# Converting weights beside a fused attention and FFN kernel: sign words and first merges of 24 blocks in PSUM instead of SBUF

## Chip, cores and metric

The kernel runs on one core of one Trainium2 chip. The metric is the device time in microseconds of one execution; of several runs the median is given. One core has the matrix engine (PE, with its weight loads as PEld), the vector engine (DVE), the scalar engine (ACT), GpSimd (POOL) and the sync engine (SP), which here issues the DMAs. Each engine works through its own instructions in order and waits on semaphores. SBUF is the large on-chip memory; PSUM has eight banks of 2 KB per partition, into which PE writes its products, and which DVE and ACT can read and write too.

## The reference

The first half is attention over 8 batches with 8 heads, 512 local and 32 global tokens, and heads of 64. A global query sees every key; a local query sees the 32 global keys and the local keys within 32 positions. The result, 4608 tokens of 512 numbers, goes through a gated FFN:

```python
k_all = np.concatenate([k_g, k_l], axis=2)
out_g = np.matmul(sm(scale * q_g @ k_all^T), v_all)
s_ll = np.where(np.abs(pos[:, None] - pos[None, :]) <= 32, scale * q_l @ k_l^T, -1e9)
out_l = np.matmul(sm(concat([scale * q_l @ k_g^T, s_ll])), concat([v_g, v_l]))
...
gate = 1.0 / (1.0 + np.exp(-(x @ w_gate)))
val = x @ w_val
return (gate * val @ w_out).astype(np.float32)
```

w_gate and w_val are 512 x 1536, w_out is 1536 x 512. All three arrive as 64-bit floating-point numbers.

## The kernel before

**Tiling.** Tokens are worked in ten chunks: the first batch in two halves of 256 tokens (chunks 0 and 1), each further batch as one chunk of 512, and all global tokens as a last chunk of 256. For each chunk attention computes x, by units of two 128-row query blocks of one head (local_unit) and one unit of 32 global queries per head (global_unit). A unit is a chain over PE, DVE and ACT: scores (L237, L317), their negated maximum and masking on DVE (L251, L322), exp on ACT (L254, L326), scaling by the reciprocal sum (L225 on DVE, L223 on ACT; p_buf, p_first and pg_buf are the scaled scores), transposes on PE (L268, L335), and products with v (L290, L291, L348).

The FFN (ffn_stream) has one item per chunk and per slice f of 128 of the 1536 inner columns: twelve matmuls each for gate and value (L380; three products of a high and a low part over four row tiles), the gate function on ACT and DVE (L388 to L399), a split of the result in a high part on ACT (L401) and a low part on POOL (L402), and the output products (L415), which collect in the PSUM banks bank_o0 to bank_o3 over all twelve f. Chunk 0 collects in bank_o0 and bank_o1, chunk 1 in bank_o2 and bank_o3, a chunk of 512 in all four. The other four banks (tag att) are for everything else. The items come in this order: eight of chunk 0 (f from 0 to 7), eight of chunk 1, the rest of both in turn, then the whole chunks.

**The weight blocks.** The 64-bit weights are converted on the chip, in 36 blocks: for each f one block of w_gate (number 3f), one of w_val (3f + 1) and one of w_out (3f + 2), each of 128 partitions x 512 numbers. A block's raw words come by DMA into one of three staging buffers; one of two buffers v takes the 32-bit result. Of each number there is a low and a high word, lying side by side, so the operations read with a step of two. On a block there are, in convert:

- L140, DVE: the sign bit of the high word into v ("sign words" below)
- L146 on DVE or L144 on ACT, in turn: the high word scaled in place, which puts the exponent right
- L147, DVE: the low word shifted right and merged into v ("first merge")
- L148, DVE: the high word shifted left and merged into v ("second merge")
- L149, ACT: the high part of v, rounded, into the weight tile
- L150, POOL: v minus the high part, the low part

Since there are two buffers v, a block's L140 waits until POOL has done L150 of the block two before. The staging buffer is free for the next load after the second merge.

**What sets the order.** A list of events with times in units of FFN work (att_events, CONVERT, START) gives the order in which the program is written; the compiler's scheduler then arranges each engine's instructions by readiness, so the order on an engine also follows the lengths it expects. Blocks of f = 0 come during the attention of chunk 0, the others at four units per f.

At the start PE has nothing to multiply for some time and runs filler matmuls (fill, L113) into a tile in bank_o3: eight, and then one at a unit's steps of chunk 0. One filler has two records in the trace.

Of the kernel before, what the change touches and what calls it, by code (L numbers as in the profile page):

```python
# [10 lines left out]
U32 = mybir.dt.uint32  # L11
AF = mybir.ActivationFunctionType
ALU = mybir.AluOpType
# [4 lines left out]
P = 128  # L18
# [12 lines left out]
DM = 512  # L31
# [25 lines left out]
def kernel(ctx, tc, qk, v, w_gate, w_val, w_out, out_l, out_g):  # L57
    nc = tc.nc
# [12 lines left out]
    ps = ctx.enter_context(tc.tile_pool(name="ps", bufs=1, space=PSUM))  # L71
# [53 lines left out]
    def stage(i):  # L125
        if i < len(w_src):
            src = w_src[i]
            st = conv_bufs[0][i % len(conv_bufs[0])].rearrange("p (t n) -> p t n", t=src.shape[1])
            nc.sync.dma_start(st, src)

    def convert(i, hi, lo):

        src = w_src[i]
        t, n = src.shape[1], src.shape[2] // 2
        st, v = (o[i % len(o)].rearrange("p (t n) -> p t n", t=t) for o in conv_bufs)
        words = st.rearrange("p t (n two) -> p t n two", two=2)
        low, high = words[:, :, :, 0], words[:, :, :, 1]
        vf, hf = v.bitcast(F32), high.bitcast(F32)
        with tc.issue_after(anchor[0].ins) if i < 3 else nullcontext():
            nc.vector.tensor_scalar(v, high, 0x80000000, None, op0=ALU.bitwise_and)  # L140


            if REBASE[i % len(REBASE)] == "s":
                nc.scalar.mul(hf, hf, 2.0 ** -112)  # L144
            else:
                nc.vector.tensor_scalar(hf, hf, 2.0 ** -112, None, op0=ALU.mult)  # L146
            nc.vector.scalar_tensor_tensor(v, low, 29, v, op0=ALU.logical_shift_right, op1=ALU.bitwise_or)  # L147
            nc.vector.scalar_tensor_tensor(v, high, 3, v, op0=ALU.logical_shift_left, op1=ALU.bitwise_or)  # L148
        nc.scalar.copy(hi, vf)  # L149
        nc.gpsimd.tensor_tensor(lo, vf, hi.bitcast(F32), op=ALU.subtract)  # L150
        stage(i + len(conv_bufs[0]))

    def convert_w(f, i):
        fs = slice(f * P, (f + 1) * P)
        w = (wg, wv)[i]
        convert(3 * f + i, w[0][:, :, fs], w[1][:, :, fs])

    def convert_wo(f):
        hi, lo = (spl.tile([P, 1, DM], F32R, name=nm, tag="kl") for nm in ("wo_hi", "wo_lo"))
        convert(3 * f + 2, hi, lo)  # L160
        nc.sync.dma_start(wo_dram[f][:, 0], hi[:, 0].bitcast(F32))
        nc.sync.dma_start(wo_dram[f][:, 1], lo[:, 0].bitcast(F32))
# [420 lines left out]
```

## Time and profile before

| | us |
|---|---|
| median of three runs | 1246.45 |
| lowest and highest | 1245.38 and 1247.57 |
| the profiled execution | 1240.82 |
| its span, from first to last instruction | 1238.9 |
| PE busy in the span | 1216.7 (98%) |
| DVE busy | 845.0 (68%) |
| ACT busy | 780.6 (63%) |
| POOL busy | 564.2 (46%) |

All durations and places quoted below are from the one profiled execution; its times count from the start of the span. Busy time counts instructions from start to end, with whatever they wait for once they have begun. PE's ends are modelled from a pipeline, so that a full PE isn't always a PE at its peak; the granted clock tells at which rate it was allowed to run. An engine's instruction can be recorded up to some 0.08 us before the previous one has ended, so starts tell how fast a queue moves. A line number such as L140 is that of the kernel before; in the changed kernel the lines behind the edit stand six further down (L140 is L146 there, L147 and L148 are L153 and L154).

### The profile page before, as it was taken

What the parts mean: (1) busy time and instruction counts of PE and PEld (TensorE: products, weight loads), DVE (VectorE), ACT (ScalarE), POOL (GpSimd) and SP (SyncE); (2) the same over time, 40 slices, a digit from 0 to 9 for tenths busy, and PEclk for the clock granted to TensorE, in tenths of its full rate; (3) what the DMA queues carried; (4) which work ended last, traced back from release to release, by engine and by line L of the source; (5) the groups of instructions that cost most, each with busy time, mean ns of one, the idle gap of its engine ahead of it and who ended that gap; (6) DMA issues with size and microseconds to landing.
All of it is one profiled execution on the core that took longest, in us unless ns stands there. A gap on an engine that the chain in (4) does not pass through costs nothing.

```text
span 1238.9 us, 20551 instructions
## 1 busy us (share of the span) xinstructions
PE 1216.7 (98%) x6884; PEld 998.4 (81%) x6884; DVE 845.0 (68%) x2433; ACT 780.6 (63%) x1899; POOL 564.2 (46%) x573
## 2 busy tenths in 40 slices
PE   8898999999999999999999999999999999999998
PEld 6677778888888788888888888888888788888897
DVE  6899976757776777767776777767776777622232
ACT  4786777756765676656765776657675666533333
POOL 2345455635554455535554555535554555311111
PEclk9898999999999999999999999999999999999999
DMA  6778754333433433433333333333433332121243
GB/s 228 230 261 251 252 169 135 110 99 96 112 90 111 131 98 100 112 118 110 94 109 107 107 105 110 94 115 109 110 93 124 106 97 81 52 93 61 68 137 120
DMA packets 59498, 151.90 MB, mean 123 GB/s; under 512 B 6144, under 2 KB 19456, under 8 KB 59392
## 3 DMA queue, kind: packets, MB, share of 16 engines
q1 hardware_dynamic: 59392, 150.59, 40.5%
q8 instruction: 54, 0.88, 0.3%
q14 instruction: 52, 0.43, 0.1%
HBM read 135.36 MB, written 15.20 MB: 122 GB/s over the span
## 4 chain that ended last, share of the span: by engine, by line
PE 82%; DVE 8%; issue 5%; ACT 2%; POOL 2%; DMA 0%; POOLq 0%; DVEq 0%; ACTq 0%
PE bank_v L380 21%; PE bank_g L380 20%; PE bank_o L415 20%; PE bank_x L237 5%; PE bank_y L268 5%; PE bank_x L348 2%; DVE p_buf L225 2%; PE bank_x L317 2%; PE bank_y L335 2%; PE bank_x L298 2%; PE bank_x L299 2%; DVE xt L148 1%; POOL hh L402 1%; PE bank_x L290 1%; DVE pt L280 1%
## 5 line engine op out<-in xcount | busy, mean ns | idle before, releaser
L380 PE MATMUL bank_g<-xt,wg 128*128 128x512 f32 (+1 forms) x1440 | 337.1, 369 | 0.9 <-DVE th L399 0.5
L380 PE MATMUL bank_v<-xt,wv 128*128 128x512 f32 (+1 forms) x1440 | 334.7, 370 | 0.2 <-ACT pg_buf L326 0.2
L415 PE MATMUL bank_o<-wo,hh 128*128 128x512 f32 x1224 | 334.3, 404 | 0.4 <-ACT hh L401 0.4
L380 PEld LDWEIGHTS bank_v<-xt,wv 128*128 128x128 f32 x1440 | 238.5, 191 | 38.7 <-issue 2.0
L380 PEld LDWEIGHTS bank_g<-xt,wg 128*128 128x128 f32 x1440 | 236.6, 190 | 40.1 <-issue 3.2
L415 PEld LDWEIGHTS bank_o<-wo,hh 128*128 128x128 f32 x1224 | 215.0, 189 | 38.2 <-ACT hh L401 0.9
L402 POOL TENSOR_TENSOR hh<-th,hh 128x512 fp32r<-128x512 f32 (+1 forms) x120 | 137.9, 1149 | 212.1 <-ACT hh L401 198.1
L254 ACT ACTIVATE s_sb<-s_sb,nm 128x224 f32<-128x224 f32 x240 | 113.7, 474 | 90.8 <-DVE nm L251 90.4
L225 DVE TENSOR_SCALAR p_buf<-s_sb,r 128x128 f32<-128x128 f32 (+1 forms) x443 | 157.7, 401 | 8.0 <-PE bank_y L268 4.5
L206 POOL TENSOR_TENSOR kl<-qk_raw,qk_hi 128x704 fp32r<-128x704 f32 x52 | 88.3, 1698 | 135.1 <-ACT qk_hi L205 135.1
L393 DVE TENSOR_SCALAR mn<-bank_g 128x512 f32<-128x512 f32 (+1 forms) x108 | 67.2, 622 | 103.0 <-ACT th L388 101.5
L388 ACT ACTIVATE th<-bank_g 128x512 f32<-128x512 f32 (+1 forms) x120 | 63.4, 528 | 95.1 <-PE bank_g L380 92.3
L401 ACT CAST hh<-th 128x512 fp32r<-128x512 f32 (+1 forms) x120 | 66.6, 555 | 89.0 <-DVE th L399 89.0
L303 POOL TENSOR_TENSOR x<-t 64x256 f32<-64x256 f32 x104 | 76.2, 733 | 99.7 <-DVE t L302 96.5
L398 DVE TENSOR_TENSOR bank_v<-bank_v,mn 128x512 f32<-128x512 f32 (+1 forms) x120 | 73.3, 611 | 44.4 <-PE bank_v L380 37.7
L251 DVE CUSTOM_DVE_ANT_0 s_sb<-bank_x,masks 128x224 f32<-128x224 f32 x240 | 84.3, 382 | 19.8 <-PE bank_x L237 15.6
L218 POOL TENSOR_TENSOR vhl<-v_raw,vhl 128x512 fp32r<-128x512 f32 x52 | 67.7, 1301 | 59.0 <-ACT vhl L217 58.1
L205 ACT CAST qk_hi<-qk_raw 128x1248 fp32r<-128x1248 f32 x52 | 64.1, 1233 | 36.6 <-PE bank_y L319 36.5
L208 POOL TENSOR_TENSOR qk_hi<-qk_raw,qk_hi 64x256 fp32r<-64x256 f32 x104 | 82.6, 814 | 4.1
L268 PE MATMUL bank_y<-ident,p_buf 128*128 128x128 f32 x496 | 78.3, 279 | 5.8 <-DVE p_buf L225 4.0
L268 PEld LDWEIGHTS bank_y<-ident,p_buf 128*128 128x128 f32 x496 | 58.6, 141 | 28.3 <-ACT pg_buf L326 9.4
L280 DVE TENSOR_TENSOR pt<-bank_y,pt 128x512 fp32r<-128x512 f32 x104 | 70.5, 678 | 14.7 <-ACT pt L279 14.7
(111 smaller groups left out, 1940.7 us busy)
## 6 DMA issues: line engine op xcount, KB each, us to landing
wo<-wo_dram SPq DMA_DIRECT2D x116, 512.0 KB, 3.6
qk_raw<-in_qk_dram SPq DMA_DIRECT2D x104, 312.0 KB, 4.3
v_raw<-in_v_dram SPq DMA_DIRECT2D x52, 256.0 KB, 2.6
out_dram<-ob SPq DMA_DIRECT2D x34, 256.0 KB, 2.7
xt<-in_w_gate_dram SPq DMA_DIRECT2D x12, 512.0 KB, 4.7
xt<-in_w_val_dram SPq DMA_DIRECT2D x12, 512.0 KB, 4.7
xt<-in_w_out_dram SPq DMA_DIRECT2D x12, 512.0 KB, 4.7
v_nat<-in_v_dram SPq DMA_DIRECT2D x8, 512.0 KB, 4.6
```

What stands on the lines that cost most here:

```text
L206: nc.gpsimd.tensor_tensor(kl, t[:, K0:Q1], hi[:, K0:Q1].bitcast(F32), op=ALU.subtract)
L208: nc.gpsimd.tensor_tensor(hi[64:128, r], t[64:128, r], hi[64:128, r].bitcast(F32), op=ALU.subtract)
L225: nc.vector.tensor_scalar(out, in_, by, None, op0=ALU.mult)
L251: anchor[0] = nc.vector.tensor_tensor_reduce(out=s_sb[:, i], in0=s_ps[:, i, 0:WIN], in1=masks[:, m], scale=-0.125, scalar=3.0e38, op0=ALU. ...
L254: nc.scalar.activation(s_sb[:, i], s_sb[:, i], AF.Exp, bias=nm[:, i:i + 1], scale=-1.0, accum_out=sm[:, i:i + 1])
L268: nc.tensor.transpose(pt_ps[:, 2 * i + t], pb[:, i, t * P:(t + 1) * P], ident)
L280: nc.vector.tensor_tensor(pt[:, 1], pt_ps, pt[:, 0].bitcast(F32), op=ALU.subtract)
L303: nc.gpsimd.tensor_tensor(dst, t0[:, :, 0], t0[:, :, 1], op=ALU.add)
L380: nc.tensor.matmul(acc, w[a][:, t, fs], xt[:, c, t, x0:x0 + ntok], start=n == 0, stop=n == 11)
L398: nc.vector.tensor_tensor(acc, acc, mn, op=ALU.mult)
L402: nc.gpsimd.tensor_tensor(hh[:, 1, 0:ntok], th, hh[:, 0, 0:ntok].bitcast(F32), op=ALU.subtract)
L415: nc.tensor.matmul(o_ps[t], ph[:, a, t * P:(t + 1) * P], pwo[:, c], start=f2 == 0 and i == 0, stop=f2 == NF - 1 and i == 2)
```

## The change

For the first 24 blocks (f from 0 to 7) a tile u of one PSUM bank is taken, bank_o2 for even and bank_o3 for odd blocks. The sign words go into u, the first merge reads and writes u, and the second merge reads u and writes v in SBUF. The in-place scaling, ACT's and POOL's steps and the other twelve blocks are as before.

```diff
         with tc.issue_after(anchor[0].ins) if i < 3 else nullcontext():
-            nc.vector.tensor_scalar(v, high, 0x80000000, None, op0=ALU.bitwise_and)
+            if i < 24:
+                u = ps.tile([P, DM], U32, name="bank_o%d" % (2 + i % 2)).rearrange("p (t n) -> p t n", t=t)
+            else:
+                u = v
+            nc.vector.tensor_scalar(u, high, 0x80000000, None, op0=ALU.bitwise_and)
...
-            nc.vector.scalar_tensor_tensor(v, low, 29, v, op0=ALU.logical_shift_right, op1=ALU.bitwise_or)
-            nc.vector.scalar_tensor_tensor(v, high, 3, v, op0=ALU.logical_shift_left, op1=ALU.bitwise_or)
+            nc.vector.scalar_tensor_tensor(u, low, 29, u, op0=ALU.logical_shift_right, op1=ALU.bitwise_or)
+            nc.vector.scalar_tensor_tensor(v, high, 3, u, op0=ALU.logical_shift_left, op1=ALU.bitwise_or)
```

Only the second merge now waits for the buffer v. A new wait is that odd blocks share bank_o3 with the filler matmuls, and that the first output products of chunk 1 need both banks back.

The scheduler arranges the first part of the program anew (some 800 of PE's 6600 instructions, up to about 170 us); from there on every engine has the same order as before.

On PE, in chunk 0's attention, the filler matmuls stand in threes before (L113; L268 are transposes, L237 scores of the next unit):

```order
L291 MATMUL bank_x<-pt_first,v_nat 64x128
L268 MATMUL bank_y<-ident,p_buf 128x128 x4
L237 MATMUL bank_x<-qk_nat 128x224 x2
L113 MATMUL bank_o_127<-ident 128x128 x3
L290 MATMUL bank_x<-pt_nat,v_nat 64x128
L291 MATMUL bank_x<-pt_nat,v_nat 64x128
```

The same place now (L297, L274, L243 and L296 are the lines L291, L268, L237 and L290 from above):

```order
L297 MATMUL bank_x<-pt_first,v_nat 64x128
L113 MATMUL bank_o_127<-ident 128x128 x8
L274 MATMUL bank_y<-ident,p_buf 128x128
L243 MATMUL bank_x<-qk_nat 128x224
L274 MATMUL bank_y<-ident,p_buf 128x128 x3
L243 MATMUL bank_x<-qk_nat 128x224
L296 MATMUL bank_x<-pt_nat,v_nat 64x128
```

The last eight fillers come in one piece, ahead of the transposes of p_buf, and block 1's sign words wait for them on DVE.

On DVE, at the beginning of the FFN, block 6 and the beginning of block 7 (L251, L257 and L258 are attention's maximum and reciprocal sum; mn, bank_v and th belong to the gate, mg to the global unit):

```order
L147 SCALAR_TENSOR_TENSOR xt<-xt 128x512
L148 SCALAR_TENSOR_TENSOR xt<-xt 128x512
L393 TENSOR_SCALAR mn<-bank_g 128x256
L257 TENSOR_SCALAR r<-sm 128x2
L140 TENSOR_SCALAR xt<-xt 128x512
L258 RECIPROCAL r<-r 128x2
L322 TENSOR_REDUCE mg<-bank_x 32x1
L225 TENSOR_SCALAR p_buf<-s_sb,r 128x128
L323 TENSOR_REDUCE mg<-bank_y 32x1
L398 TENSOR_TENSOR bank_v<-bank_v,mn 128x256
L324 TENSOR_SCALAR mg<-mg 32x1
L399 SCALAR_TENSOR_TENSOR th<-th,bank_v 128x256
```

And now (six lines further down; bank_o_696 is block 6's u, bank_o_739 block 7's):

```order
L153 SCALAR_TENSOR_TENSOR bank_o_696<-xt,bank_o_696 128x512
L399 TENSOR_SCALAR mn<-bank_g 128x256
L264 RECIPROCAL r<-r 128x2
L328 TENSOR_REDUCE mg<-bank_x 32x1
L231 TENSOR_SCALAR p_buf<-s_sb,r 128x128
L329 TENSOR_REDUCE mg<-bank_y 32x1
L404 TENSOR_TENSOR bank_v<-bank_v,mn 128x256
L330 TENSOR_SCALAR mg<-mg 32x1
L405 SCALAR_TENSOR_TENSOR th<-th,bank_v 128x256
L154 SCALAR_TENSOR_TENSOR xt<-xt,bank_o_696 128x512
L146 TENSOR_SCALAR bank_o_739<-xt 128x512
```

Block 6's second merge and block 7's sign words have moved behind the gate's operations. The following blocks, up to the 24th, likewise stand some ten attention and FFN rows later in DVE's queue than before; by the 30th the order is the same again.

## The prediction

> **What bounds the kernel now.** I read the page's slices first, then the busy time by stretch, then the lines and the chain of waits inside the stretch that the change touches. The slices give one tenth of the busy share per digit, 31 us each:
>
> ```profile
> PE   8898999999999999999999999999999999999998
> DVE  6899976757776777767776777767776777622232
> ```
>
> PE is full nearly everywhere, and only in the first six slices is DVE full as well. Those are the slices in which the weight blocks are converted. From the sixth slice on DVE has a quarter or more to spare, and the changed kernel has the same order of instructions there. So what the change is worth is decided before 170 us, by how much PE idles there. The busy time in four stretches (columns: stretch, its length, then PE, PEld, DVE, ACT and POOL busy, the granted clock):
>
> ```profile
> 16.00:44.00 28.00, 23.32 (x120) 17.46 (x121) 24.22 (x73) 17.31 (x46) 10.26 (x9) 0.83 0.58 180
> 44.00:88.00 44.00, 42.80 (x281) 32.58 (x281) 38.52 (x116) 34.74 (x110) 19.28 (x16) 0.95 0.77 253
> 88.00:122.00 34.00, 30.37 (x200) 24.26 (x197) 31.82 (x76) 24.32 (x72) 15.57 (x13) 0.90 0.79 248
> 122.00:170.00 48.00, 45.12 (x287) 35.37 (x287) 47.32 (x113) 33.83 (x95) 24.08 (x19) 0.96 0.78 243
> ```
>
> The 24 changed blocks lie in the first three. In 44 to 88 us PE is busy 42.8 of 44 us and DVE has 5.5 us free: PE sets the pace. In 88 to 122 us it is DVE, with 2.2 us free while PE idles 3.6 us; in 122 to 170 us DVE has 0.7 us free. A DVE delay left over at 122 us is therefore still there at 170 us.
>
> The sign words' line in 16 to 122 us (count, total and mean, then the idle time before it and what ended it):
>
> ```profile
> L140 DVE TENSOR_SCALAR xt<-xt 128x512 uint32<-128x512 uint32 x24 | 10.8, 451 | 2.3 <-POOL wv L150 1.2 <-POOL wo_lo L150 1.1
> ```
>
> Its mean is above what it takes undisturbed. The spread of single instructions shows why (minimum, median, maximum in ns): the sign words, the first merge, and three FFN operations that have one input in PSUM:
>
> ```profile
> L147 DVE SCALAR_TENSOR_TENSOR xt<-xt x24: 657/685/1656, 17.5 to 120.0; 128x512 uint32<-128x512 uint32 x24
> L140 DVE TENSOR_SCALAR xt<-xt x24: 393/416/940, 16.7 to 119.3; 128x512 uint32<-128x512 uint32 x24
> L399 DVE SCALAR_TENSOR_TENSOR th<-th,bank_v x120: 400/666/690, 51.3 to 1231.9; 128x512 f32<-128x512 f32 x84, 128x256 f32<-128x256 f32 x36
> L398 DVE TENSOR_TENSOR bank_v<-bank_v,mn x120: 399/681/700, 50.8 to 1231.3; 128x512 f32<-128x512 f32 x84, 128x256 f32<-128x256 f32 x36
> L393 DVE TENSOR_SCALAR mn<-bank_g x108: 391/672/693, 48.2 to 1230.3; 128x512 f32<-128x512 f32 x84, 128x256 f32<-128x256 f32 x24
> ```
>
> Merges with both inputs in SBUF go up to 1656 ns; operations of that size with a PSUM operand never pass 700 in 120 calls. What the long ones wait for is seen by laying DVE's and POOL's timelines side by side (start, duration):
>
> ```profile
> 111.36 1.66 DVE L147 SCALAR_TENSOR_TENSOR xt<-xt 128x512 uint32<-128x512 uint32 x1
> 113.12 1.04 DVE L148 SCALAR_TENSOR_TENSOR xt<-xt 128x512 uint32<-128x512 uint32 x1
> 115.59 1.64 DVE L148 SCALAR_TENSOR_TENSOR xt<-xt 128x512 uint32<-128x512 uint32 x1
> 120.80 1.25 DVE L148 SCALAR_TENSOR_TENSOR xt<-xt 128x512 uint32<-128x512 uint32 x1
> 111.02 1.46 POOL L150 TENSOR_TENSOR wo_lo<-xt,wo_hi 128x512 fp32r<-128x512 f32 x1
> 112.44 1.17 POOL L402 TENSOR_TENSOR hh<-th,hh 128x256 fp32r<-128x256 f32 x1
> 114.89 1.79 POOL L150 TENSOR_TENSOR wg<-xt,wg 128x512 fp32r<-128x512 f32 x1 [1.28 <-ACT wg L149]
> ```
>
> Each of the first three merges begins inside a POOL subtraction and ends about 0.55 us after it: DVE and POOL exclude each other while both work on SBUF, and the loser waits inside its instruction, where it counts as busy. The fourth is the last merge of the 24 blocks.
>
> **The change, step by step.**
>
> *The sign words.* L140 goes from SBUF to SBUF in a median of 416 ns. No row writes PSUM from SBUF with one input. From below the bound is 416 (the rate is kept), from above 693 (L393, the same form and size, which reads PSUM and is not faster than 0.67 at 512 columns). I take 0.68, the nearest row in which PSUM is an operand.
>
> *The merges.* The first has one input in SBUF and one in PSUM, and so has the second. L398 and L399 have that shape and stay between 0.66 and 0.70, so I take 0.68 without waits. The waits that go are in these busy times by stretch, of L140, L147 and L148 in that order:
>
> ```profile
> 16.00:44.00 28.00, 2.93 (x7) 0.83 0.58 180
> 44.00:88.00 44.00, 4.60 (x10) 0.95 0.77 253
> 88.00:122.00 34.00, 3.26 (x8) 0.90 0.79 248
> ...
> 16.00:44.00 28.00, 4.99 (x6) 0.83 0.58 180
> 44.00:88.00 44.00, 7.04 (x10) 0.95 0.77 253
> 88.00:122.00 34.00, 6.58 (x8) 0.90 0.79 248
> ...
> 16.00:44.00 28.00, 4.92 (x6) 0.83 0.58 180
> 44.00:88.00 44.00, 6.48 (x9) 0.95 0.77 253
> 88.00:122.00 34.00, 7.96 (x9) 0.90 0.79 248
> ```
>
> Sign words, 24 in all, 7 + 10 + 7 (one straddles 88 us): 4.76 - 2.93 = +1.8, 6.80 - 4.60 = +2.2, 4.76 - 3.26 = +1.5 us. Merges, 12 + 19 + 17 of them: 8.16 - 9.91 = -1.75, 12.92 - 13.52 = -0.6, 11.56 - 14.54 = -3.0 us. Together +0.1, +1.6 and -1.5 us: nearly nothing in total, but with the cost where PE sets the pace and the gain where DVE does. Of the +1.6 I count half, 0.8, because DVE's 5.5 us of free time there are not all where an instruction stands ready (ends 0 and 1.6).
>
> L399 at most takes 690, about the median 685 of a merge in SBUF alone (its own median, 666, mixes two widths). [...]
>
> *The wait for the buffer.* L140 waited 1.2 and 1.1 us for POOL to finish with the buffer that it overwrites. That wait moves to the second merge, behind about 1.2 us of sign words and first merge, which covers it. The first of the two (43.3 us) lay beside PE's first gate products and is worth nothing; the second (87.6 us) opens the DVE stretch: -1.1 us (ends 0 and -2.3).
>
> *The filler matmuls.* They share bank_o3, so they now all come ahead of block 1's sign words: eight in a row stand in front of the transposes of p_buf.
>
> ```profile
> 23.44 0.96 PE L113 MATMUL bank_o<-ident 128*128 128x128 f32 x6
> 28.39 0.94 PE L113 MATMUL bank_o<-ident 128*128 128x128 f32 x6
> 35.56 0.46 PE L268 MATMUL bank_y<-ident,p_buf 128*128 128x128 f32 x2 [2.24 <-DVE p_buf L225]
> ```
>
> Three take 0.95 us (two records each), so five more cost 1.6 us there, and the three at 28.4 us are gone: +0.6, half of it absorbed by PE's 2.24 us wait for DVE at 33 to 35 us: +0.3 us. Block 1's sign words, waiting for PE, hold up block 2's second merge and the scaling of p_first behind them; block 2's first ones were put ahead. Ends: 0 and 1.5 us.
>
> *The order.* From block 6 on DVE's queue has a block's work later among the attention and FFN rows. The row of the place shown above (block 6's second merge and block 7's sign words behind L399 rather than ahead of it) reads:
>
> ```profile
> 48.18 0.42 DVE L393 TENSOR_SCALAR mn<-bank_g 128x256 f32<-128x256 f32 x1 [0.59 <-ACT th L388]
> 49.92 0.68 DVE L322 TENSOR_REDUCE mg<-bank_x 32x1 f32<-32x512 f32 x1 [0.84 <-PE bank_x L317]
> ```
>
> One merge and one L140, 0.69 + 0.42 = 1.1 us, ran ahead of these two waits; now DVE stands idle instead and does that work later, when it is full. +1.1 us (ends 0 and 1.8, with the first merge too).
>
> *What costs nothing:* the first product into bank_o2 and bank_o3 now waits for blocks 22 and 23, whose last merge ends at 122 us. The first chunk's eight items put 48 products ahead of it, and the 49th is issued 30 us after that merge, which is the cover:
>
> ```profile
> 152.30 0.73 PE L415 MATMUL bank_o<-wo,hh 128*128 128x512 f32 x2
> ```
>
> SP issues the blocks' loads in their order as before.
>
> Sum: +0.1 + 0.8 - 1.5 - 1.1 + 0.3 + 1.1 = -0.3 us. The profiled execution took 1240.82 us, span 1238.9, and would take 1240.5; it was 5.6 us below the median of the runs shown, 1246.45, which becomes 1246.1.
>
> **The rivals.** A measurement of this kernel can tell about 0.2%, 2.5 us, from no change.
>
> *Faster, the chain of the third stretch.* The chain of waits there runs through exactly these merges and POOL's subtraction:
>
> ```profile
> 111.36 1.67 DVE xt L147
> 113.12 1.05 DVE xt L148
> 114.89 1.79 POOL wg L150
> 110.46 0.46 PE L335 MATMUL bank_y<-ident,pg_buf 32*128 32x32 f32 x5 [1.77 <-DVE pg_buf L225]
> 110.00:120.00 10.00, 9.16 (x47) 7.95 (x48) 8.71 (x17) 4.96 (x15) 6.68 (x6) 0.66 0.81 273
> ```
>
> If the subtraction also drops to its unhindered 1.28 us (-0.5) and PE, no longer held up, keeps its full clock where 0.66 was granted (9.16 us of PE work at 0.66 is 6.0 at 1.00; I count most of it, -2.9), the time is 1246.1 - 3.4 = 1242.7. Against it: PE's longest wait there, 1.77 us, is for attention's pg_buf, not for a weight block. 0.21.
>
> *Faster, the sign words keep their rate.* At 0.416 instead of 0.68 the steps lose 0.26 x 7, half of 0.26 x 10 and 0.26 x 7: -5.0, 1241.1. Only the missing row speaks for it. 0.07. [...]
>
> *Slower, the waits only move.* POOL's subtractions remain, 43% of the time to 122 us (45.1 of 106), and DVE still has operations in SBUF alone, such as L225 on pg_buf, which takes 500 ns undisturbed and up to 1253:
>
> ```profile
> L225 DVE TENSOR_SCALAR pg_buf<-pg_buf,mg x64: 500/693/1253, 53.8 to 1071.3; 32x576 f32<-32x576 f32 x64
> ```
>
> If the wait that a merge no longer takes is taken by the next such operation, the 24 sign words are paid and nothing is gained for them. With share s moved, the merges give back 1.75 s + 0.3 s + 3.0 s = 5.0 s us: 1251.1 with s = 1. It decides from 2.8 us, s over 0.56; with filler and order at their upper ends (+1.9), from s over 0.2. For it: a POOL operation is over only when it is over, whichever DVE instruction comes next. Against it: sign word and two merges follow each other with few rows between, so 1.3 us of POOL mostly pass beside them. 0.29.
>
> *A dearer merge from PSUM.* By rows it costs at most 700 - 657 = 43 ns on each of 48 merges, +2.1, 1248.2, within 0.2%. The medians speak against it. 0.04. [...]
>
> **How the numbers follow.** The forecast has 0.39 and the time, 1246.1; its own range, with the two largest ends on each side (order and wait; filler and the second stretch's half), is 1243.8 to 1248.1. Faster by over 0.2%: 0.21 + 0.07 = 0.28. Within: 0.39 + 0.04 = 0.43. Slower: 0.29. The range goes from 1242.0 to 1250.5, which leaves out the kept rate and the last part of moved waits, under 0.2 together.
>
> **What would show it.** In the changed profile: the sign words at 0.67 to 0.69 us, both merges without any over 0.75, their maxima gone; L225 and the rescaling on DVE with means as before (higher would be the moved waits); DVE's busy time to 122 us within 1 us of 94.6; PE's idle time before 170 us as now. Sign words at 0.42, or merges still over 1 us, would make the steps wrong; an end of the conversion more than 3 us away from now, the time.

## The result and the profile after

The changed kernel takes 1261.7 us (median of 4 runs, 1259.0 to 1262.0), the kernel before 1247.0 us beside it. The ratio is 1.0121, with a 95% interval of 1.0102 to 1.014: slower by 1.2%, where no change was forecast, and outside the range. The profiled execution took 1259.01 us, span 1257.1.

The page's slices of the changed kernel, PE and DVE:

```profile
PE   8899889999999999999999999999999999999998
DVE  6786896857777677767776777767776877632232
```

From the seventh slice on the digits differ by one at most. The difference lies before, where DVE, once 9 in the third to fifth slices, now has 8, 6 and 8. The same four stretches as in the prediction:

```profile
16.00:44.00 28.00, 22.33 (x125) 16.77 (x123) 22.66 (x75) 17.14 (x47) 8.65 (x8) 0.88 0.56 175
44.00:88.00 44.00, 42.32 (x263) 31.52 (x262) 35.01 (x105) 30.95 (x100) 14.05 (x14) 0.92 0.65 209
88.00:122.00 34.00, 30.90 (x185) 22.88 (x183) 25.66 (x67) 20.92 (x66) 11.52 (x11) 0.80 0.69 220
122.00:170.00 48.00, 40.65 (x226) 32.01 (x225) 41.65 (x97) 32.04 (x86) 22.92 (x19) 0.86 0.72 226
```

DVE's busy time in 88 to 122 us fell from 31.8 to 25.7 us, and still PE got less done there: 185 matmul records for 200. The clock column (the first behind POOL's) is where to look: 0.80 for 0.90, and 0.86 for 0.96 behind it. The operations themselves came out as forecast (lines of the changed kernel; minimum, median and maximum in ns):

```profile
L146 DVE TENSOR_SCALAR bank_o<-xt x24: 671/677/695, 17.8 to 137.1; 128x512 uint32<-128x512 uint32 x24
L146 DVE TENSOR_SCALAR xt<-xt x12: 405/417/1489, 139.0 to 181.1; 128x512 uint32<-128x512 uint32 x12
L153 DVE SCALAR_TENSOR_TENSOR bank_o<-xt,bank_o x24: 661/683/697, 19.0 to 139.9; 128x512 uint32<-128x512 uint32 x24
L154 DVE SCALAR_TENSOR_TENSOR xt<-xt,bank_o x24: 656/675/689, 21.2 to 140.8; 128x512 uint32<-128x512 uint32 x24
L231 DVE TENSOR_SCALAR pg_buf<-pg_buf,mg x64: 499/721/1925, 55.4 to 1089.6; 32x576 f32<-32x576 f32 x64
```

Sign words cost 0.68 us, no merge of the 24 blocks waits for POOL any more, and the rescaling of pg_buf, the place where a moved wait would show, has a median 28 ns higher over all 64 times. In the first 185 us alone its mean did rise, from 759 ns (11 times) to 1001 (10 times), while that of the 128-column p_buf beside it fell from 735 to 400. Yet the 24th block's second merge starts at 140.8 us instead of 120.8.

How the lost time divides can be read from one row of each kernel, PE to 185 us. The kernel before:

```profile
0.00:185.00 185.00, 168.81 (x1059) 131.43 (x1060) 156.21 (x435) 129.07 (x376) 78.54 (x76) 0.94 0.73 232
```

And the changed one:

```profile
0.00:185.00 185.00, 163.07 (x948) 124.83 (x949) 145.35 (x400) 115.38 (x335) 67.17 (x69) 0.88 0.68 219
```

PE idles 21.9 us instead of 16.2, +5.7. And to 185 us the changed kernel runs at half clock for 44.4 us instead of 23.9, in four periods each, which is another 10.2 us of full speed (the clock column, 0.88 for 0.94, is rounded and gives 11.1). Together 15.9 us; the span grew by 18.2. So by this estimate nearly two thirds of the loss is not waiting, but work at a lower clock.

Windows cut at the clock's own steps show what goes ahead of it (three of the changed kernel's four periods; length, PE, PEld, DVE, ACT, POOL, clock):

```profile
95.10:98.50 3.40, 2.25 (x18) 1.60 (x18) 3.38 (x11) 3.24 (x10) 1.67 (x2) 1.00 1.06 384
98.50:108.70 10.20, 10.20 (x38) 7.17 (x37) 5.49 (x19) 3.69 (x14) 1.04 (x2) 0.50 0.46 142
...
115.60:119.00 3.40, 1.53 (x6) 0.64 (x5) 3.37 (x8) 1.46 (x4) 2.87 (x3) 1.00 0.70 275
119.00:125.80 6.80, 6.80 (x35) 5.80 (x34) 2.81 (x5) 2.35 (x7) 1.27 (x1) 0.50 0.57 170
156.50:159.90 3.40, 1.73 (x12) 1.13 (x11) 3.40 (x7) 2.59 (x5) 1.98 (x3) 1.00 0.61 171
159.90:173.60 13.70, 11.72 (x44) 9.28 (x43) 13.66 (x29) 7.92 (x23) 7.78 (x6) 0.50 0.81 251
```

Before each half-clock period stands a window of 3.4 us in which PE idled for 1.15 to 1.9 us (2.4 us before the one not shown, from 37.1 to 50.7 us). The period lasts two to four such lengths (6.8 to 13.7 us), PE full or not. And in the first two of those shown DVE is busy for only 5.5 of 10.2 and 2.8 of 6.8 us: it waits for PE, and its conversion work comes later, when it is full. What DVE's masking waited for PE's scores between 16 and 170 us (us in total, times, longest), first in the kernel before, then in the changed one:

```profile
DVE s_sb L251 <- PE bank_x L237: 1.7, 4, 0.8
...
DVE s_sb L257 <- PE bank_x L243: 13.0, 5, 4.5
```

The kernel before has four such periods too, but shorter ones (this is the one at 113 us, with the window ahead of it):

```profile
109.60:113.00 3.40, 2.16 (x23) 2.04 (x24) 3.37 (x4) 1.63 (x5) 3.40 (x4) 0.99 1.00 347
113.00:119.80 6.80, 6.80 (x25) 5.76 (x25) 5.55 (x13) 3.42 (x11) 3.69 (x3) 0.50 0.71 234
```

The fourteen traces of this case, cut in windows of 3.4 us up to 185 us, tell more. Of the windows at full clock, all 27 in which PE idled 1.70 us or more, which is about half of a window, were followed by half clock; so were 21 of the 88 with 0.58 to 1.70 us, and none of the 480 with less. Between the two no sharp limit shows: half clock followed 0.86 us of idle time in the kernel before (the window from 20.8 to 24.2 us) and did not follow 1.43 us in the changed kernel (142.9 to 146.3 us).

The gap in the window from 95.1 us shows how the order makes it. In the kernel before, two matmuls and a product stand between attention's output (L291) and the transposes of pg_buf (L335):

```profile
92.42 0.38 PE L291 MATMUL bank_x<-pt_nat,v_nat 128*64 128x128 f32 x2
92.73 0.50 PE L380 MATMUL bank_v<-xt,wv 128*128 128x256 f32 x2
93.07 0.39 PE L415 MATMUL bank_o<-wo,hh 128*128 128x512 f32 x1
93.95 0.47 PE L335 MATMUL bank_y<-ident,pg_buf 32*128 32x32 f32 x5 [0.50 <-DVE pg_buf L225]
```

In the changed kernel the same transposes follow at once, with nothing between:

```profile
95.88 0.38 PE L297 MATMUL bank_x<-pt_nat,v_nat 128*64 128x128 f32 x2
97.41 0.46 PE L341 MATMUL bank_y<-ident,pg_buf 32*128 32x32 f32 x5 [1.15 <-DVE pg_buf L231]
```

DVE's scaling of pg_buf takes about as long in both (1.25 and 1.29 us beside a POOL subtraction). What covered it is gone.

### The profile page after: what moved, and what is told of

The parts are those of the page before. It is cut to its first block, busy times and chain, and to the rows that moved or that the text cites. A ratio compares the mean times of both kernels' runs of the same rounds, so it can differ in the third digit from the quotient of the medians.

```text
span 1257.1 us, 20548 instructions
## 1 busy us (share of the span) xinstructions
PE 1228.2 (98%) x6884; PEld 1004.9 (80%) x6884; DVE 847.6 (67%) x2433; ACT 780.3 (62%) x1899; POOL 560.1 (45%) x573
## 4 chain that ended last, share of the span: by engine, by line
PE 80%; DVE 7%; issue 6%; POOL 3%; ACT 2%; DMA 1%; POOLq 0%; ACTq 0%; DVEq 0%
PE bank_v L386 21%; PE bank_g L386 19%; PE bank_o L421 19%; PE bank_x L243 5%; PE bank_y L274 4%; DVE p_buf L231 3%; PE bank_x L354 2%; PE bank_x L323 2%; PE bank_y L341 2%; PE bank_x L304 2%; PE bank_x L305 2%; POOL hh L408 1%; DVE pt L286 1%; PE bank_o L113 1%; DVE mg L328 1%
## 5 line engine op out<-in xcount | busy, mean ns | idle before, releaser
L231 DVE TENSOR_SCALAR p_buf<-s_sb,r 128x128 f32<-128x128 f32 (+1 forms) x443 | 154.7, 395 | 7.3 <-PE bank_y L274 3.6
L257 DVE CUSTOM_DVE_ANT_0 s_sb<-bank_x,masks 128x224 f32<-128x224 f32 x240 | 84.3, 381 | 29.3 <-PE bank_x L243 25.4
L274 PE MATMUL bank_y<-ident,p_buf 128*128 128x128 f32 x496 | 79.6, 279 | 8.6 <-DVE p_buf L231 4.0
L211 ACT CAST qk_hi<-qk_raw 128x1248 fp32r<-128x1248 f32 x52 | 64.2, 1234 | 36.8 <-PE bank_y L325 36.7
L274 PEld LDWEIGHTS bank_y<-ident,p_buf 128*128 128x128 f32 x496 | 59.1, 141 | 33.3 <-ACT pg_buf L332 9.5
```

Source lines behind the costliest of these rows:

```text
L231: nc.vector.tensor_scalar(out, in_, by, None, op0=ALU.mult)
L257: anchor[0] = nc.vector.tensor_tensor_reduce(out=s_sb[:, i], in0=s_ps[:, i, 0:WIN], in1=masks[:, m], scale=-0.125, scalar=3.0e38, op0=ALU. ...
L274: nc.tensor.transpose(pt_ps[:, 2 * i + t], pb[:, i, t * P:(t + 1) * P], ident)
```

## The experiments

Two theories stood against each other: that the loss comes from the **order** which the compile-time scheduler chose for the changed kernel, or from the **operations** in PSUM and their two buffers. A third question was how much of it is the clock.

**Order and operations apart (e1, e2).** The order of a kernel's instructions on each engine, as far as the two kernels differ (the first 803 on PE, 320 on DVE, 297 on ACT, 74 on POOL, 90 on SP), was put into a table, and each instruction tied behind the one ahead of it by a dependency for the order of issue alone:

```diff
         tile_local_global_attn_then_gated_ffn_kernel(tc, *args)
+        pin(tc)
...
+    for e, order in ORDER.items():
+        for a, b in zip(order, order[1:]):
+            tc.add_manual_dep(traced[e][b], traced[e][a].name, info, reason="order")
```

e1 has the changed operations in the old order, and the fillers moved to another bank:

```diff
-    fill_ps = ps.tile([P, DM], F32, name="bank_o3")
+    fill_ps = ps.tile([P, DM], F32, name="bank_o0")
```

> The operations of the changed kernel (24 blocks with sign words and first merge in PSUM banks bank_o2 and bank_o3), every engine pinned to the issue order of the kernel before; the filler matmuls write bank_o0, since in bank_o3 that order contradicts the change. Order theory (the loss comes from the later conversions in the new compile-time order): no loss is left, 1247 us within 3, ratio to before 0.997 to 1.003, DVE busy in 40 to 90 us as before (some 9 of each 10 us) and half-clock time back to some 24 us. PSUM theory (the operations or their buffers cost the time): 1259 to 1264 us, ratio 1.010 to 1.014, as the changed kernel. The first forecast's sum without its term for the order gives 1245 us.

Measured: 1243.3 us, ratio to the kernel before 0.9974 (0.9954 to 0.9993). The loss is gone, and a small gain stands in its place. e2 is the reverse, the kernel before in the new order:

> The operations of the kernel before (everything in SBUF), every engine pinned to the issue order of the changed kernel. Order theory: slow all the same, 1256 to 1264 us, ratio to before 1.008 to 1.014, with the 24th block's second merge at 135 us or later and half-clock time of some 40 us. PSUM theory: 1247 us within 3.

Measured: 1269.9 us, ratio 1.0203 (1.018 to 1.0225). The order alone, with not one operation changed, loses more than the whole change did, and more than was expected of it. PE to 185 us in e1:

```profile
0.00:185.00 185.00, 170.25 (x1080) 133.37 (x1081) 150.59 (x437) 130.23 (x379) 76.14 (x78) 0.94 0.73 234
```

and in e2:

```profile
0.00:185.00 185.00, 158.82 (x921) 120.78 (x921) 138.97 (x385) 111.11 (x323) 68.19 (x66) 0.87 0.66 212
```

The first merges of e2, all in SBUF:

```profile
L153 DVE SCALAR_TENSOR_TENSOR xt<-xt x36: 657/678/1774, 17.6 to 190.9; 128x512 uint32<-128x512 uint32 x36
```

In e1 PE has done 21 more records by 185 us than in the kernel before; in e2 it is 138 fewer, and the merges in SBUF still take up to 1.77 us beside POOL. The operations gain in both orders: 1245.5 to 1243.3 us in the old one, 1269.9 to 1261.7 in the new one. The operations theory falls, and the order theory holds. No run pins a kernel to its own order and changes nothing else; the nearest is e8 below (20 fillers besides), which stands where the kernel before stands, so no cost of the pinning itself is seen.

**The shared bank (e3).** The changed kernel with only the filler line of e1's diff, nothing pinned:

> The changed kernel with the filler matmuls in bank_o0 in place of bank_o3, so that they no longer share a bank with the sign words; the order is chosen anew at compile time and its blocks 7 to 28 stand a mean of 8 rows of other work later in VectorE's queue than before, against 11 in the changed kernel. Bank-sharing theory (the fillers and the sign words of bank_o3 wait for each other): the loss goes, 1247 us within 4. Order theory: the loss shrinks about with the rows, 1253 to 1260 us. PSUM theory: 1259 to 1264 us.

Measured: 1250.9 us (7 runs, 1247.8 to 1262.0), ratio 1.0053 (1.0026 to 1.0081). It is 5.4 us above the kernel before as measured beside it, and the changed kernel was 14.7 above its own. That the fillers shared bank_o3 with the sign words thus costs some 9 to 11 us, and the rest is left. It costs them by the order that follows from it: e2 has that order without the sharing, and is slow. The seven runs are of one program and differ by 14 us. The slowest was at a mean clock of 0.976, the six others at 0.986 to 0.990. Here is what happened in the slowest:

```profile
32.70:36.10 3.40, 1.00 (x5) 0.68 (x6) 3.40 (x11) 2.52 (x8) 0.85 (x2) 1.00 0.64 246
36.10:73.70 37.60, 36.73 (x137) 27.60 (x138) 21.18 (x65) 18.20 (x53) 9.97 (x9) 0.50 0.49 167
```

After a window with 2.4 us of idle time PE ran at half clock for 37.6 us, though it was busy for 36.7 of them. Taking the time lost to the clock, span x (1 - mean clock), from each of the seven leaves 1231.7 to 1236.5 us: a spread of 5 us for one of 14.

**The clock tested by itself (e4, e5).** If gaps cost more than themselves, then filling them with matmuls that do no work must make the kernel faster, although every wait stays. e5 is the changed kernel, its own order pinned, with 38 fillers at its own waits, into the bank that the waiting instruction is about to overwrite:

```diff
+    def cover(kind, dst):
+        sites[kind] = sites.get(kind, -1) + 1
+        made = [nc.tensor.matmul(dst, ident, ident, start=True, stop=True).ins
+                for _ in range(COVER[kind].get(sites[kind], 0))]
...
+                done = cover("T", pt_ps[:, 2 * i + t])
-                nc.tensor.transpose(pt_ps[:, 2 * i + t], pb[:, i, t * P:(t + 1) * P], ident)
+                done(nc.tensor.transpose(pt_ps[:, 2 * i + t], pb[:, i, t * P:(t + 1) * P], ident).ins)
```

> The changed kernel, its own order pinned, with 38 more filler matmuls of 0.275 us, which do no part of the work, where TensorE waited in its trace: at 26, 36, 53, 97, 137, 146, 153, 160, 164, 184 and 187 us (gaps of 0.43 to 3.1 us). The waits for products at 81 and 117 us can't be filled, since all eight banks are in use. Clock theory: most of the half-clock time of 44 us goes, 1247 to 1254 us, clock 0.987 to 0.992, though every wait is still in the order. Gap theory (the waits that the order makes are the loss): no change, 1259 to 1263 us. If it is neither, the fillers themselves delay the path: over 1263 us.

Measured: 1246.2 us, ratio 1.0007 (0.9991 to 1.0023), where the changed kernel has 1.0121. Its row to 185 us, and the stretch that ran at half clock in the changed kernel:

```profile
0.00:185.00 185.00, 167.22 (x1091) 129.97 (x1091) 153.51 (x424) 123.28 (x361) 73.20 (x74) 0.97 0.71 231
...
98.50:108.70 10.20, 8.10 (x61) 6.13 (x61) 9.51 (x25) 6.76 (x20) 5.38 (x5) 1.00 0.76 270
```

The clock is 0.97 for 0.88. PE does 61 records in 98.5 to 108.7 us instead of 38, and DVE is busy for 9.5 us of it instead of 5.5. e4 is the same on e1, with 20 fillers:

> e1 (the changed operations in the order of the kernel before) with 20 more filler matmuls of 0.275 us, which do no part of the work, at seven places where TensorE waited in e1's trace (gaps of 0.46 to 2.17 us, filled to less than their length). Clock theory (a gap of over some 1 us costs far more than itself, since half clock of 3.4 us and more follows): the half-clock periods at 35, 110 and 158 us go, time 1234 to 1240 us, clock 0.993 or more. Gap theory (only the waiting itself costs): 1243 to 1245 us, as e1 or a little above it.

Measured: 1235.7 us, ratio 0.992 (0.9904 to 0.9936), against e1's 1243.3. In both the gap theory falls. But the clock isn't all: e4 and e5 have the same operations and nearly the same clock, and the new order is still 10.5 us slower. That part is waiting: to 185 us PE idles 17.8 us in e5 and 13.0 in e4, and 18 more fillers, some 5 us, stand in e5's waits.

**Is it lateness in DVE's queue? (e6, e7).** The new order has blocks 7 to 28 a mean of 11 rows later in DVE's queue. If that were the harm, an earlier due time would mend it. e6 is e3 with it, e7 the kernel before with it:

```diff
-CONVERT = (-2, 4, 1, 3)
+CONVERT = (-6, 4, 1, 3)
```

> The changed kernel, fillers in bank_o0 as in e3, with the conversions due four units earlier in the kernel's own table (CONVERT -6 in place of -2); nothing pinned. Its blocks 7 to 24 stand a mean of 4 rows later in VectorE's queue than before (e3: 9), the blocks from 26 on up to 15 rows earlier. Order theory: the loss is gone, 1240 to 1248 us. If lateness in VectorE's queue isn't what costs, it stays at e3's 1251 us or above.

> Control for e6: the kernel before with the conversions due four units earlier; its first 24 blocks stand where they stood, the later ones up to 16 rows earlier. Order theory: small, 1243 to 1249 us; if the earlier due time by itself brings the gain that e6 shows, this one shows it too.

Measured: e6 1256.9 us, ratio 1.0099 (1.0076 to 1.0122); e7 1256.2 us, 1.0091 (1.0068 to 1.0113). What the order theory expected of lateness failed in both. With fewer rows of lateness e6 is no faster than e3, and in e7, whose first 24 blocks stand where they stood, the later ones moved ahead cost 9 us. Mean clocks are 0.979 to 0.985 in both. But these two runs do not rule lateness out: against e7, its control with the same due time, e6 loses only 0.7 us, where e3 lost 5.4 with twice the rows. What speaks against lateness in DVE's queue as the cause is e11, next, which puts all of that queue back in the old order and gains nothing. That leaves the waits of PE, which e5 tests.

**Which queue carries it? (e10, e11).** e3 with one engine alone pinned to the old order (the table of e1 cut to that engine):

> e3 (the changed kernel, fillers in bank_o0) with TensorE alone pinned to the order of the kernel before; the other engines' orders are chosen anew under that and differ from both. If the order of TensorE's own queue carries the loss: e1's 1243 us within 2. If VectorE's does: e3's 1251 us within 3. If it takes both: between.

> e3 with VectorE alone pinned to the order of the kernel before; TensorE's and the others' are chosen anew under that and differ from both. If the order of VectorE's queue carries the loss: 1243 us within 2. If TensorE's does: 1251 us within 3. If it takes both: between.

Measured: e10 1247.0 us, ratio 1.0009 (0.9997 to 1.0021); e11 1254.0 us, 1.0068 (1.0044 to 1.0092). PE's row to 185 us in e10:

```profile
0.00:185.00 185.00, 167.00 (x1030) 128.71 (x1031) 150.78 (x428) 125.18 (x366) 72.69 (x74) 0.93 0.71 231
```

and in e11:

```profile
0.00:185.00 185.00, 166.95 (x974) 130.79 (x974) 145.12 (x410) 119.62 (x349) 71.89 (x73) 0.87 0.69 225
```

The old order on PE brings back about half of what lies between e3 and e1, so e10 falls between what was expected of the two queues; on DVE, none. PE is busy for the same time in both and differs in the clock. It is the order of PE's own queue more than DVE's, though each run let the free engines choose anew, so this is a lean and no proof.

**Is the gain of e4 the change's or the fillers'? (e8, e12, e9).** e8 gives the kernel before e4's 20 fillers:

> The kernel before, its own order pinned, with e4's 20 filler matmuls, which do no part of the work, at the same seven places. It tells the change's operations apart from the clock: e4 against e8 is the change with the order held and the half-clock periods mostly gone. If the fillers alone make e4's gain of 11 us, this one stands at 1236 us within 2; if the operations in PSUM carry the 2 to 3 us that e1 shows against the kernel before, it stands at 1238 to 1240 us; if the fillers gain nothing without the change, 1245 to 1247 us.

Measured: 1246.4 us, ratio 1.0009 (0.9992 to 1.0025). No gain, at places chosen for e1's waits. Its trace has another wait, which the kernel before, slowed by half clock there, did not have, and 17 us at half clock follow:

```profile
49.15 1.17 PE L282 MATMUL bank_y<-ident,p_buf 128*128 128x128 f32 x4 [2.25 <-ACT p_buf L236]
```

So e12 fills that one and the other waits of its own trace too (47 fillers; the expectation says 45):

> The kernel before, its own order pinned, with 45 filler matmuls, which do no part of the work, at the waits of its own trace and of e8's (22, 35, 37, 39, 49, 79, 94, 103, 110, 128, 135, 159, 161 and 168 us). It asks whether e9's 1234 us can be had without the change. If the clock is all that e4 and e9 gained: 1234 to 1238 us, clock 0.996 or more. If the operations in PSUM are needed for it, since the conversions in SBUF keep VectorE late and the waits come back elsewhere: 1241 to 1247 us, whatever the clock.

Measured: 1241.6 us, ratio 0.9971 (0.996 to 0.9983), mean clock 0.998 to 1.0. With the clock nearly full the kernel before stays over 1240 us: its loss to the clock fell by 11.2 us and its time by only 4.5, so the two are not the same. The clock alone does not make e4's gain. e9 is e4 with more fillers (33 at twelve places; the expectation says eleven):

> e4 with the fillers at eleven places instead of seven (33 in place of 20): the waits for ScalarE's copies at 35 and 39 us (0.68 us each), 50 us and 101 us are filled too, and those at 33, 109 and 156 us more fully. Clock theory: the one half-clock period that e4 has left (36 to 46 us, worth some 5 us) goes: 1230 to 1233 us, clock 0.998 or more. Gap theory: 1235 to 1238 us, since each further filler can only delay.

Measured: 1234.3 us, ratio 0.991 (0.9897 to 0.9923). The half-clock period at 36 us went, but e4 had been losing only 3.7 us to the clock in its median run, not 5, and e9's time is 1.4 us below e4's, less than was expected of it, and no more than the kernel before differed between the two (1246.7 beside e4, 1245.2 beside e9). The rows to 185 us, e12 first:

```profile
0.00:185.00 185.00, 172.30 (x1151) 135.60 (x1151) 158.34 (x434) 128.91 (x374) 78.57 (x76) 0.99 0.71 231
```

and e9:

```profile
0.00:185.00 185.00, 174.19 (x1171) 138.10 (x1172) 154.04 (x449) 133.78 (x388) 77.08 (x79) 0.99 0.73 238
```

At the same clock the changed operations leave DVE 4.3 us less busy with more done (449 records for 434), and PE 1.9 us less idle. The difference is 7.4 us here, 1241.6 against 1234.3. How much of it is the operations alone isn't shown: e12's 14 further fillers take 3.9 us, partly in waits that the operations in SBUF leave, partly perhaps on the path. Without any fillers, e1 showed 2.2 us. e9 is faster than both kernels.

The runs side by side (the clock is the middle of the runs' mean clocks, the loss the middle of span x (1 - mean clock); the kernel before is the one beside e1 to e3, 1245.2 to 1247.0 beside the others; one of e5's twelve runs, at 1250.4 us, shows a mean clock of 0.946, which its time does not bear out):

| kernel | operations | order | extra fillers | us | clock | lost to it, us |
|---|---|---|---|---|---|---|
| before | SBUF | old | none | 1245.5 | 0.990 | 12.4 |
| changed | PSUM | new | none | 1261.7 | 0.981 | 24.6 |
| e1 | PSUM | old | none | 1243.3 | 0.988 | 14.9 |
| e2 | SBUF | new | none | 1269.9 | 0.976 | 31.1 |
| e5 | PSUM | new | 38 | 1246.2 | 0.996 | 5.0 |
| e4 | PSUM | old | 20 | 1235.7 | 0.997 | 3.7 |
| e9 | PSUM | old | 33 | 1234.3 | 0.999 | 1.8 |
| e12 | SBUF | old | 47 | 1241.6 | 0.999 | 1.2 |

## Why the prediction was wrong

*The sign words* were right: 0.677 us in the median, where 0.68 was taken, against 0.417 for the twelve blocks that stay in SBUF. The rival in which they keep their rate falls.

*The merges* were right: 0.66 to 0.70 us, and no wait for POOL left among 48. The rival with a dearer merge falls with them.

*The wait for the buffer* went as said: none of the 24 second merges waited for POOL (two waited 2.2 us for ACT's scaling). The sum without the order was right in size: e1, which keeps the old order and has no lump of fillers, gives a gain of 2.2 us (0.9 to 5.7 by its interval) where those terms said 1.7 (+0.1 + 0.8 - 1.5 - 1.1).

*The filler matmuls* were priced at +0.3 us, 1.5 at most, by the time that they take themselves. The bank that they share with the sign words costs some 9 to 11 us (e3). The term counted them where they stand and not what the scheduler does with everything behind them.

*The order* is the step that failed: "+1.1 us (ends 0 and 1.8, with the first merge too)". It measures 18.4 us between e1 and the changed kernel, fillers included. It was priced at one place, by what DVE would have done there in its idle time. The rows that had moved on PE, 392 of the first 803 standing elsewhere, were not priced at all. And a wait of PE was taken at its own length, which the trace of before already spoke against: its row with 0.66 granted in 110 to 120 us, behind a wait of 1.77 us, was used in a rival for the gain alone.

*The slower rival* had the side right and the mechanism wrong. Its price, 5.0 us, would have been paid by operations like the rescaling of pg_buf. In the first 185 us of the changed kernel that paid some 2.4 us more (10 times 1001 ns instead of 759), but the 128-column p_buf paid some 4 us less, and in e1, with the same operations in the old order, the rescaling has a mean of 732 ns, and in e2, with the old operations in the new order, 1041. So the merges' waits did not move on; what pg_buf took came with the order.

*What would show it* listed "PE's idle time before 170 us as now". It rose (in 88 to 170 us from 6.5 to 10.5 us), which tells of the failure; the granted clock, which tells of more of it, was not on the list. *The reading of the slices* was loose as well: DVE is at 9 in the third to fifth slices only, not in the first six, and a 7 leaves a fifth to spare and not a quarter.

What stays open: which moves in PE's queue do the most harm, since e10 and e11 also moved the other engines, and what ends a half-clock period, which lasted one window in some places and eleven in e3. Nor is it shown that lateness in DVE's queue costs nothing beside the order on PE (e6, e7).

## What to carry to other kernels

Where a scheduler orders the program at compile time, an edit to some operations is also an edit to the order of all of them: price the moved rows on the engine that sets the end, or pin the old order and measure the operations alone. Waits of TensorE can cost the work at half clock behind them as well as themselves (here behind all 27 windows of 3.4 us of which they made up half, and behind 21 of 88 from 0.6 us on), so read the clock column beside the idle time. And before an edit is given up as slow, try it in the order of the kernel before: this one was worth 0.2% there, and with fillers in the waits 0.9%, of which fillers alone brought the kernel before 0.3%.

## What the runs showed of the hardware

- In these traces TensorE's clock fell to half, for one to eleven times 3.4 us, behind a 3.4 us window in which it idled: up to 185 us, behind all 27 windows with 1.70 us of idle time or more, 21 of 88 with 0.58 to 1.70 us, none of 480 with less. In e3 it stayed there for 37.6 us with PE busy 98% of the time. Runs of one program differ: e3's by 14 us, e1's by 10.6 us (1235.1 us at a mean clock of 0.996, 1245.7 at 0.986).
- A DVE operation of two inputs with one in PSUM did not wait for POOL once in 48 (697 ns at most); with both in SBUF it took up to 1774 ns in e2. The price was on the sign words, 0.26 us each: this operation of one input took 0.677 us into PSUM and 0.417 into SBUF.
